# A mixed attention kernel on one core: score banks in groups of two instead of three and two, reciprocals moved to GpSimd, and a re-planned order of work

## The chip, the core and the metric

The kernel runs on one core of a Trainium2 chip, whose engines work side by side: TensorE (PE; its weight loads are PEld), VectorE (DVE), ScalarE (ACT), GpSimd (POOL) and SyncE (SP, which issues DMAs). TensorE writes into PSUM, which has eight banks of 512 float32 columns over 128 partitions. The metric is the device time of one execution in microseconds (us), as a median over runs.

## What is computed

Two attention branches over the same input x (2048 tokens, width 512, 32 heads of 16) are mixed by a gate. All data is bfloat16.

```python
g = sigmoid((x * gate_w).sum(-1, keepdims=True))
# branch A: softmax attention, per head, 2048 x 2048 scores
q, k, v = split(x @ A_wqkv)
a = (softmax(q @ k.T * 16 ** -0.5) @ v) @ A_wo
# branch B: linear attention with a feature map, per head
q, k, v = split(x @ B_wqkv)
phi = lambda t: concat(softmax(t @ w_phi), softmax(-(t @ w_phi)))
num = phi(q) @ (phi(k).T @ v)
den = phi(q) @ phi(k).sum(tokens) + 1e-6
b = (num / den) @ B_wo
out = g * a + (1 - g) * b
```

## The kernel before

**Branch A** is nearly all of the time. Its scores are cut into 2048 tiles of 128 keys x 512 queries of one head. Four heads lie in the four 32-row strips of TensorE, so a *pack* is the four tiles of one key block; there are 512 packs, and 16 packs in a row (all keys) make one *group* `g` of four heads and 512 queries. Each tile is scored (`_scores`, one matmul in one row strip, L931), exponentiated, and multiplied with the values (`_values`, one matmul in one column strip, L1034), where an extra column of ones gives the softmax denominators. All tiles of a group add into one PSUM bank `ot`.

The exponentials are shared between two engines. `NUMS` says how many tiles of each group go to VectorE (452 in all). ScalarE takes the rest (1596) as ACTIVATE with Exp (`_exp`, L978), out of a *ring* of PSUM banks (`NRING` = 5, banks 0 to 4). The groups of the ring alternate between three banks and two (`GROUPS` = (3, 2)). The score pass of ring group k (`_qk`) waits for the exponential k-2, which used the same banks. The first tiles go in two halves of 256 queries, so that ScalarE can start on half of the input. VectorE's tiles (`_vector_batch`, four at a time) are scored into banks of the *pool* (banks 5 to 7), turned into the bits of an exponential by one TENSOR_SCALAR each (L847), and refined by two additions for each batch (L864, one of 2048 columns and one of 4096). Each of these tiles costs four value matmuls instead of one, against `V` and a scaled copy `V2`.

A finished group is normalized in `_norm`: a transpose out of PSUM (L1055), multiplication of the denominators with the gate (L1062), reciprocal (L1064), product (L1067, on GpSimd where two groups go together, which is 15 times), transpose back (L1072).

**Branch B** is done in between, in `_branch_b`. `_b_pair` handles two token tiles at a time, 16 times: projections, a copy out of PSUM (L1160), negation (L1179), a tree of maxima (L1181, L1182), subtraction (L1184), exponential on ScalarE (L1187), a tree of sums (L1189, L1190, last L1192), reciprocal (L1200, `_b_rec`) and product (L1194). `_b_kv` sums keys with values, `_b_num` multiplies with the query features and divides (L1266, L1269, L1270, all VectorE). Projections of branch A (`_proj_k`, `_proj_q`, `_proj_v`, and for the first 512 tokens `_proj_k0`, `_proj_q0`) take pool banks too, except for the very first key and query projection, which go to banks 3 and 4. Query tiles are masked into two halves by GpSimd (L728), `V2` is made there too (L766).

**The order of the work** is made by a planner (`Plan`). Each operation has an engine, an estimated cost, a due time `prio`, an earliest time `rel` and dependencies; `order` goes through time and gives the next free engine the ready operation of least rank, with pool banks handed out on the way. The result is one fixed list for each engine; each engine then works its list strictly in order and waits on semaphores. `LAT` and `MORE` are the assumed delays between engines. An operation whose `urgent` time has come goes ahead of all others (`rank`). PE operations that would delay the next score pass are held back (`_late`). A score pass in the row strips can take along scores of VectorE's tiles in strips that are free (`_beside`). Where PE would be too idle, the planner inserts filler passes with zeros (`pad`, `filler`, L1041) and whole-array fillers ahead of score passes (L950, from score pass number 8 on); `SPAN`, `SHARE`, `GAPS`, `FLOOR`, `PAD` set when. Operations of GpSimd, and those of VectorE listed in `PORT`, are planned never to overlap.

Of the kernel before, what the change touches and what calls it, by code (L numbers as in the profile page):

```python
# [63 lines left out]
class Plan:  # L64
# [3 lines left out]
    MORE = {("ACT", "PE"): 0.09, ("ACT", "DVE"): 0.1, ("DVE", "PE"): 0.022}  # L68
# [3 lines left out]
    SPAN, SHARE, FILL = 2.4, 0.5, 0.2155  # L72
    PAD, PADS, OVER = 0.45, 2, 0.2
    SLIP, GAPS, FLOOR = 0, 0.6, 0.44
# [76 lines left out]
    NEAR = 0.2  # L151
    SAME = 16
    OPEN = 99
    HURRY, FREE = 20, 60
    PORT = ("v_step", "b_neg", "b_max", "b_sub", "b_sum", "b_mul", "n_mul", "n_den", "kvbd")
# [227 lines left out]
class _Kernel:  # L383
    NRING = 5
    GROUPS = (3, 2)
    NSLOT = 25
# [4 lines left out]
    KEEP = 15  # L391
    URGENT, AHEAD, SOON, REST = 5, -(1 << 30), 4, 6
    QDUE, KDUE, VDUE = 24, 17, 8
    P_Q, P_MUL, P_NEG = 1, 1, 0
    GDUE = 26
    VMIN = 12
    ALONE, EARLY = 9, 8
# [30 lines left out]
    def _memory(self, ctx):  # L428
# [13 lines left out]
        self.iden = sb("iden", [P, P], BF16)  # L442
# [3 lines left out]
        self.zero = sb("zero", [P, 32], BF16)  # L446
        self.warm = sb("warm", [P, QCH], BF16)
        self.gwb = sb("gwb", [P, 4, P], BF16)
        self.gh = sb("gh", [P, 2, NQC, 16], F32)
# [20 lines left out]
        self.bq = sb("bq", [P, self.NBQ, 2, 2 * D], BF16)  # L470
        self.btree = sb("btree", [P, 32, 8, 4], BF16)
        self.bsum = sb("bsum", [P, P], F32)
        self.brec = sb("brec", [P, P], FP16)
        self.kvacc = sb("kvacc", [P, 2, 260], F32)
# [71 lines left out]
    def _consts(self):  # L546
# [25 lines left out]
        op("POOL", lambda e: e.memset(self.zero[:], 0.0), 0.1, writes=[self.b_zero], prio=-75)  # L572
        self.b_wphi0 = B()
# [14 lines left out]
    def _projections(self):  # L588
# [12 lines left out]
        for j in range(NQC):  # L601
            if j == 0:
                for half, banks in enumerate(((3, 4), (None, None))):
                    self._proj_k0(half, banks[0])
                    self._proj_q0(half, banks[1])
            else:
                self._proj_k(0, j)
            self._proj_v(0, 4 * j)
            self._proj_v(0, 4 * j + 2)
# [63 lines left out]
    def _proj_k0(self, half, bank):  # L673
# [4 lines left out]
                   self.c_dve(256), 2 * half - 2.5, -99, "kproj", [self.b_k0[half]], n=256, bank=bank)  # L678

    def _proj_q0(self, half, bank):  # L680
# [4 lines left out]
        for c in range(4):  # L685
# [3 lines left out]
                   acquire=None if c else pool)  # L689
        for side in range(2):  # L690
# [48 lines left out]
    def _proj_v(self, pr, t0):  # L739
# [5 lines left out]
        for tt in range(2):  # L745
# [8 lines left out]
            mm.urgent = 64 * pr + t0 - self.SOON + 2  # L754
# [53 lines left out]
    NUMS = (4, 10, 12, 14, 14, 14, 14, 14, 14, 14, 14, 14, 15, 14, 16, 14, 13, 14, 15, 14, 17, 14, 15, 15, 14, 14, 11, 15, 21, 16, 21, 12)  # L808
# [134 lines left out]
    def _qk(self, a, b, half=None):  # L943
# [22 lines left out]
        o.pad = k >= 8  # L966
# [83 lines left out]
    def _norm(self, qc, src, side, last, dst, b_dst, due, job, alone=False):  # L1050
# [6 lines left out]
        if not (side or alone):  # L1057
# [4 lines left out]
        op("DVE", lambda e: e.tensor_tensor(rinv[:, lo:hi], den, h, ALU.mult), 0.23, reads=reads + [self.b_g],  # L1062
           writes=[b_rinv], name="n_den", prio=due)
        op("DVE", lambda e: e.reciprocal(rinv[:, lo:hi], rinv[:, lo:hi]), 0.2 + 0.1 * n, reads=[b_rinv],  # L1064
           writes=[b_rinv], name="n_rec", prio=due)
        spare = self.P_MUL and n == 2
        op("POOL" if spare else "DVE", lambda e: e.tensor_tensor(  # L1067
# [8 lines left out]
    NDUE = 26  # L1076
    K0, SK, Q0, SQ = 34.0, 12.0, 214.0, 14.25

    def _branch_b(self):
# [7 lines left out]
        self.b_kvbd, self.b_onB, self.b_rinvB = B(), [B(), B()], [B(), B()]  # L1087
        self.b_phiT = [B() for _ in range(4)]
# [58 lines left out]
    def _b_pair(self, s, t0, due):  # L1147
# [25 lines left out]
        def chain(ops, off, bufs):  # L1173
            for name, cost, fn in ops:
                spare = self.P_NEG and name == "b_neg"
                op("POOL" if spare else "DVE", fn, 1.35 if spare else cost, reads=bufs, writes=bufs, name=name,
                   prio=due + off)
        spread = lambda t: t[:, :, None, :].to_broadcast([P, 32, DH, 4])
        chain([("b_neg", 0.16 + 1024 * 0.00027, lambda e: e.tensor_scalar(both[:, :, 1], both[:, :, 0], -1.0, 0.0,  # L1179
                                                                         op0=ALU.mult, op1=ALU.add)),  # L1180
# [10 lines left out]
                                                                       half[:, :, n:2 * n], ALU.add)) for n in (4, 2)]  # L1191
              + [("b_sum", 0.3, lambda e: e.tensor_tensor(last(self.bsum[:]), half[:, :, 0], half[:, :, 1], ALU.add)),  # L1192
                 ("b_rec", 0.96, self._b_rec),
                 ("b_mul", two(2048), lambda e: e.tensor_tensor(x, x, spread(last(self.brec[:])), ALU.mult))],  # L1194
              2, [b, self.b_tree])
        return slot

    def _b_rec(self, e):
        with self.nc.allow_low_precision(reason="11 bits, each product is rounded to 8"):
            return e.reciprocal(self.brec[:], self.bsum[:])  # L1200
# [47 lines left out]
    def _b_num(self, t, due):  # L1248
# [4 lines left out]
        b_rinv.readers = []  # L1253
        for hf in range(2):
            job = Job()

            def mm(e, hf=hf, job=job):
# [6 lines left out]
            view = self._view17(job)  # L1264
            r = rinv[:, 16 * hf:16 * hf + 16]
# [7 lines left out]
                prio=due - 20, release=job))  # L1273
        b_rinv.readers = list(muls)
# [26 lines left out]
    def _out(self, qc):  # L1301
        op, NT, NQC = self.plan.op, self.NT, self.NQC
        for tt in range(4):
# [5 lines left out]
            if final:  # L1309
                due = self.NPACK  # L1310
                deps = (self.last_bits if tt < 2 else [self.pvs[-1]]) + [w for b in b_onTA[:3] for w in b.writers]
            else:
                deps = [w for b in b_onTA for w in b.writers]
            for x in first:
                x.prio, x.rel = due, due - (6 if not final else 8 if tt < 2 else 0)
                x.deps += deps
            m = first[-1]
# [58 lines left out]
```

## Time and profile before the change

| | |
|---|---|
| median of three runs | 772.22 us (771.98 to 772.43) |
| the profiled execution's own time | 772.22 us |
| its span, first to last instruction | 770.2 us |
| TensorE clock granted | 1.000 throughout |
| exponentials on ScalarE (L978) | 641: 318 of three banks, 318 of two, 5 small ones |
| exponentials of branch B on ScalarE (L1187) | 16 |
| tiles on VectorE (L847) | 452 |
| filler matmuls (L1041) | 760 |
| GpSimd busy | 57.9 us |

A page of the profile gives for each engine its busy time, share of the span and number of instructions; then groups of instructions by source line, as engine, operation, output<-inputs, shapes and count, followed by busy time, mean length of one in ns, idle time before them and what ended it. The chain that ended last is followed back from the last instruction: at each step to what released it or, where nothing did, to the instruction before it on its engine. A ScalarE instruction begins before the one ahead of it has ended, so the spans of neighbours overlap, and an engine may look busy while it waits.

### The profile page before, as it was taken

To read this page: it belongs to the slowest core of one execution; us is meant where nothing else is said; L and a number is where in the kernel's file an instruction comes from. 1 tells how busy PE (TensorE), PEld (TensorE's weight loads), DVE (VectorE), ACT (ScalarE), POOL (GpSimd) and SP (SyncE) were. 2 spreads that over 40 slices of the span, in tenths; PEclk is the share of its full clock that TensorE was granted. 3 is DMA by queue.
4 is the path that set the end of the run, shared out by engine and by line. 5 is a ranking of instruction groups with operands and counts; after the bars stand their busy time and mean duration, and the time that the engine had idled before them with its cause. 6 is when DMAs were issued, how large, how long until landed. Compare 5 with 4: busy or idle time off the path is not lost.

```text
span 770.2 us, 16369 instructions
## 1 busy us (share of the span) xinstructions
PE 747.0 (97%) x7126; PEld 231.5 (30%) x7126; DVE 725.3 (94%) x1207; ACT 755.1 (98%) x663; POOL 57.9 (8%) x73
## 2 busy tenths in 40 slices
PE   8999999999999999999999999999999999999998
PEld 4333333322322232222232223222323232322222
DVE  4789999999999999999999999999999999999994
ACT  6999999999999999999999999999999999999996
POOL 3200102000010100001001010000010101010000
PEclk9999999999999999999999999999999999999999
DMA  9510000000000000000111010102001110100000
GB/s 233 124 29 1 2 1 2 1 1 2 1 1 2 1 2 1 1 2 1 29 28 29 21 35 15 42 9 49 8 9 36 32 31 16 35 9 2 1 2 28
DMA packets 46456, 16.79 MB, mean 22 GB/s; under 512 B 40752, under 2 KB 45872, under 8 KB 46384
## 3 DMA queue, kind: packets, MB, share of 16 engines
q1 hardware_dynamic: 44512, 14.97, 9.1%
q8 instruction: 55, 0.90, 0.5%
q10 hardware_dynamic: 1872, 0.79, 0.4%
q14 instruction: 17, 0.14, 0.1%
HBM read 4.21 MB, written 2.10 MB: 8 GB/s over the span
## 4 chain that ended last, share of the span: by engine, by line
ACT 87%; PE 7%; DVE 5%; DMA 1%; SPq 0%; issue 0%
ACT ET L978 83%; ACT bq L1187 4%; PE ps L931 2%; PE ps L1034 2%; PE ps L640 2%; DVE vs L847 2%; DVE vs L864 1%; DMA xT<-in_A_x_dram 1%; DVE WB L1133 0%; DVE bq L1184 0%; PE ps L1041 0%; DVE bq L1160 0%; DVE btree L1182 0%; PE ps L749 0%; DVE ghB L802 0%; SPq L515 0%
## 5 line engine op out<-in xcount | busy, mean ns | idle before, releaser
L978 ACT ACTIVATE ET<-ps 128x1024 bf16<-128x1024 f32 (+2 forms) x641 | 725.7, 1340 | 2.4 <-PE ps L931 2.4
L931 PE MATMUL ps<-qT,kT 32*128 32x512 bf16 (+1 forms) x2053 | 304.9, 383 | 12.8 <-ACT ET L978 8.2
L847 DVE TENSOR_SCALAR vs<-ps 128x512 uint16<-128x512 f32 x452 | 297.4, 681 | 13.6 <-PE ps L931 11.9
L864 DVE TENSOR_SCALAR vs<-vs 128x2048 uint16<-128x2048 uint16 x226 | 214.8, 955 | 0.8
L1034 PE MATMUL ps<-ET,V 128*32 128x512 bf16 x1596 | 196.7, 387 | 0.1
L1034 PE MATMUL ps<-vs,V 128*32 128x512 bf16 x1808 | 179.9, 384 | 2.9 <-DVE vs L864 2.7
L931 PEld LDWEIGHTS ps<-qT,kT 32*128 32x128 bf16 x2053 | 76.9, 91 | 261.0 <-ACT ET L978 187.1
L1034 PEld LDWEIGHTS ps<-ET,V 128*32 128x32 bf16 x1596 | 49.9, 94 | 92.6 <-issue 79.7
L1041 PE MATMUL ps<-kT,zero 128*32 128x512 bf16 x760 | 75.1, 383 | 0.0
L1034 PEld LDWEIGHTS ps<-vs,V 128*32 128x32 bf16 x1808 | 45.1, 95 | 67.7 <-issue 31.3
L640 PE MATMUL ps<-WB,xT 128*128 128x512 bf16 x192 | 56.7, 384 | 0.4 <-DVE WB L1133 0.4
L728 POOL TENSOR_SCALAR qT<-qtmp,mask 128x512 bf16<-128x512 bf16 x30 | 25.6, 865 | 311.2 <-DVE qtmp L723 311.2
L1067 POOL TENSOR_TENSOR T<-T,rinv 128x512 bf16<-128x512 f32 x15 | 16.5, 1102 | 296.7 <-DVE rinv L1064 296.7
L640 PE MATMUL ps<-xT,WA 128*128 128x512 bf16 x120 | 35.8, 384 | 0.0
L1187 ACT ACTIVATE bq<-bq 128x2048 bf16<-128x2048 bf16 x16 | 31.5, 1970 | 0.4 <-DVE bq L1184 0.3
L1055 DVE STREAM_TRANSPOSE T<-ps 128x512 f32<-128x512 f32 x32 | 22.7, 710 | 7.7 <-PE ps L1034 7.2
L1041 PEld LDWEIGHTS ps<-kT,zero 128*32 128x32 bf16 x760 | 19.4, 95 | 18.9 <-issue 13.7
L1160 DVE CAST bq<-ps 128x512 bf16<-128x512 f32 x32 | 21.7, 683 | 2.2 <-PE ps L640 2.2
L640 PEld LDWEIGHTS ps<-WB,xT 128*128 128x128 bf16 x192 | 14.1, 97 | 27.3 <-issue 16.4
L1184 DVE TENSOR_TENSOR bq<-bq,btree 128x2048 bf16<-128x2048 bf16 x16 | 19.8, 1240 | 0.1
L1194 DVE TENSOR_TENSOR bq<-bq,brec 128x2048 bf16<-128x2048 bf16 x16 | 19.6, 1224 | 0.0
L640 PE MATMUL ps<-WoA,onTA 128*128 128x512 bf16 x64 | 18.7, 382 | 0.0
(75 smaller groups left out, 341.2 us busy)
## 6 DMA issues: line engine op xcount, KB each, us to landing
WB<-in_B_wqkv_dram SPq DMA_DIRECT2D x1, 1536.0 KB, 8.7
out_dram<-WB SPq DMA_DIRECT2D x12, 128.0 KB, 1.7
WA<-in_A_wqkv_dram SPq DMA_DIRECT2D x2, 384.0 KB, 4.5
WoB<-in_B_wo_dram SPq DMA_DIRECT2D x1, 512.0 KB, 3.8
WoA<-in_A_wo_dram SPq DMA_DIRECT2D x1, 512.0 KB, 4.8
WA<-in_A_wqkv_dram ACTq DMA_DIRECT2D x2, 128.0 KB, 3.0
WA<-in_A_wqkv_dram ACTq DMA_DIRECT2D x1, 256.0 KB, 4.2
WA<-in_A_wqkv_dram SPq DMA_DIRECT2D x1, 256.0 KB, 5.0
```

The source lines that it names most:

```text
L640: return e.matmul(out, lhs, rhs, start=start, stop=stop)
L728: x = self.plan.op("POOL", lambda e, side=side: e.tensor_scalar(self.qT[:, s0 + side, :], tmp, self.mask[:, side:side + 1], 0.0, op0=ALU.m ...
L847: parts.append(op("DVE", lambda e, j=j, job=job: e.tensor_scalar(va[:, 0, j, :], self._bank(job), SCALE * LOG2E * 128.0, float(ORIGIN), op ...
L864: o = op("DVE", lambda e, k=k, src=src, dst=dst: e.tensor_scalar(dst, src, float(STEPS[k - 1]), None, op0=ALU.add), 0.16 + k * n * QCH * 0 ...
L931: return e.matmul(out[:, cols], self.kT[32 * i:32 * i + 32, cp, kt * TOK:(kt + 1) * TOK], self.qT[32 * i:32 * i + 32, s, cols], start=True ...
L978: o = plan.op("ACT", lambda e: e.activation(self.ET[:, a % NS:a % NS + n, cols], self.ps[:, a % NR:a % NR + n, cols], ACT.Exp, scale=SCALE ...
L1034: ins = e.matmul(self._bank(ot)[32 * i:32 * i + 32, :], v[:, v0:v0 + 32], tile, start=(kt == 0), stop=(kt == self.NT - 1), tile_position=( ...
L1041: ins = e.matmul(self._bank(ot)[32 * i:32 * i + 32, :], self.zero[:], self.kT[:, 0, 0:QCH], start=False, stop=False, tile_position=(0, 32 ...
L1055: t1 = op("DVE", lambda e: e.transpose(T1[:, side].rearrange("p b s -> p (b s)"), src()), 0.735, deps=last, writes=[b_T1[side]], name="n_t ...
L1160: [lambda e, b, k=k: e.tensor_copy(bq[:, k].rearrange("p (g s v) -> p g s v", g=8, s=2)[:, :, 0, :], b.rearrange("p (g v) -> p g v", g=8))],
L1184: + [("b_sub", two(2048), lambda e: e.tensor_tensor(x, x, spread(tree[:, :, 0]), ALU.subtract))],
L1187: op("ACT", lambda e: e.activation(flat, flat, ACT.Exp), 1.8, reads=[b], writes=[b], name="b_exp", prio=due + 1)
```

## The change

- The ring shrinks from five banks to four, in groups of two and two; the pool has banks 4 to 7. The slots that hold exponentiated tiles are 24 instead of 25. The first four tiles, not five, go in halves. The very first key and query projections land in banks 3 and 2.
- `NUMS` gives VectorE 466 tiles.
- `_reciprocal` is new: seven GpSimd instructions (a first guess from the bits, then two rounds of multiply, scale-and-add, multiply). It replaces VectorE's reciprocal in `_b_pair` and, where two groups are normalized together, in `_norm`, where the product with the gate (L1062) moves to GpSimd too.
- In `_b_pair` the negation and the last sum (now `b_total`) run on GpSimd. With `P_SUM = 1` the two middle sums stay on VectorE, since the condition is `n <= P_SUM` for n of 4 and 2. With `P_BMUL = 0` the product stays as well.
- With `P_M = 0` the new GpSimd branch of `_b_num` isn't taken. `PADK = 8` is the score pass from which fillers may precede scores, as before. `LAST`, `FIRST_OUT`, `NEXT_OUT` and `DEP_OUT` have the values that the code had.
- `_proj_k0` and `_proj_q0` get an `urgent` time, so that the first keys and queries go ahead of other projections.
- Many numbers of the planner differ: delays (`MORE`), thresholds for fillers, due times of branch B, of the gate and of projections; `SAME` (the preference for staying in TensorE's row or column mode) goes from 16 to 100.

```diff
-    MORE = {("ACT", "PE"): 0.09, ("ACT", "DVE"): 0.1, ("DVE", "PE"): 0.022}
+    MORE = {('ACT', 'PE'): 0.21, ('ACT', 'DVE'): 0.1, ('DVE', 'PE'): 0.022, ('PE', 'DVE'): 0.027}
-    SPAN, SHARE, FILL = 2.4, 0.5, 0.2155
-    PAD, PADS, OVER = 0.45, 2, 0.2
-    SLIP, GAPS, FLOOR = 0, 0.6, 0.44
+    SPAN, SHARE, FILL = 3.0, 0.48, 0.2155
+    PAD, PADS, OVER = 0.45, 2, 0.1
+    SLIP, GAPS, FLOOR = 0, 0.7, 0.3
-    NEAR = 0.2
-    SAME = 16
+    NEAR = 0.1
+    SAME = 100
-    HURRY, FREE = 20, 60
+    HURRY, FREE = 10, 50
-    NRING = 5
-    GROUPS = (3, 2)
-    NSLOT = 25
+    NRING = 4
+    GROUPS = (2, 2)
+    NSLOT = 24
-    KEEP = 15
-    URGENT, AHEAD, SOON, REST = 5, -(1 << 30), 4, 6
+    KEEP = 13
+    URGENT, AHEAD, SOON, REST = 5, -(1 << 30), 6, 4
-    P_Q, P_MUL, P_NEG = 1, 1, 0
-    GDUE = 26
+    P_Q, P_MUL, P_NEG = 1, 1, 1
+    P_REC, P_SUM = 1, 1
+    P_M, P_BMUL, CHUNKS = 0, 0, 8
+    GDUE = 36
-    ALONE, EARLY = 9, 8
+    VSOON = 4
+    PADK = 8
+    LAST, FIRST_OUT, NEXT_OUT, DEP_OUT = 0, 8, 0, 2
+    ALONE, EARLY = 12, 5
...
-                for half, banks in enumerate(((3, 4), (None, None))):
+                for half, banks in enumerate(((3, 4) if self.NRING == 5 else (3, 2), (None, None))):
...
-                   self.c_dve(256), 2 * half - 2.5, -99, "kproj", [self.b_k0[half]], n=256, bank=bank)
+                   self.c_dve(256), 2 * half - 2.5, -99, "kproj", [self.b_k0[half]], n=256, bank=bank,
+                   urgent=3 * half - 99)
...
+            m.urgent = half - 99
...
-            mm.urgent = 64 * pr + t0 - self.SOON + 2
+            mm.urgent = 64 * pr + t0 - self.VSOON
...
-    NUMS = (4, 10, 12, 14, 14, 14, 14, 14, 14, 14, 14, 14, 15, 14, 16, 14, 13, 14, 15, 14, 17, 14, 15, 15, 14, 14, 11, 15, 21, 16, 21, 12)
+    NUMS = (4, 8, 12, 14, 14, 14, 17, 14, 14, 14, 14, 14, 17, 14, 16, 16, 13, 18, 15, 12, 18, 16, 17, 13, 16, 17, 9, 20, 22, 16, 15, 13)
...
-    NDUE = 26
-    K0, SK, Q0, SQ = 34.0, 12.0, 214.0, 14.25
+    NDUE = 23
+    K0, SK, Q0, SQ = 30.0, 12.0, 217.0, 14.25
...
+    def _reciprocal(self, s, guess, tmp, out, reads, bufs, prio):
+
+        n = s.shape[-1]
+        high = lambda a: a.bitcast(U16).rearrange("p (n two) -> p n two", two=2)[:, :, 1]
+        t, r = tmp[:, 0], tmp[:, 1]
+        do = lambda name, cost, fn: self.plan.op("POOL", fn, cost, reads=reads, writes=bufs, name=name, prio=prio)
+        do("r_bits", 0.17 + 0.001 * n, lambda e: e.tensor_scalar(
+            high(guess), high(s), -1.0, float(0x7EE0), op0=ALU.mult, op1=ALU.add))
+        for x, y, by, plus in ((guess, r, -1.2011100358638287, 2.192845599791731), (r, out, -1.0, 2.0)):
+            do("r_mul", 0.17 + 0.0019 * n, lambda e, x=x: e.tensor_tensor(t, s, x, ALU.mult))
+            do("r_rest", 0.17 + 0.001 * n, lambda e, by=by, plus=plus: e.tensor_scalar(
+                t, t, by, plus, op0=ALU.mult, op1=ALU.add))
+            do("r_step", 0.17 + 0.0019 * n, lambda e, x=x, y=y: e.tensor_tensor(y, x, t, ALU.mult))
```

## The prediction

> **What bounds the kernel now.** I read the page's busy times first, then the chain that ended last, then the groups of instructions, and only then the starts of single instructions.
>
> ```profile
> PE 747.0 (97%) x7126; PEld 231.5 (30%) x7126; DVE 725.3 (94%) x1207; ACT 755.1 (98%) x663; POOL 57.9 (8%) x73
> ...
> ACT 87%; PE 7%; DVE 5%; DMA 1%; SPq 0%; issue 0%
> ACT ET L978 83%; ACT bq L1187 4%; PE ps L931 2%; PE ps L1034 2%; PE ps L640 2%; DVE vs L847 2%; DVE vs L864 1%; DMA xT<-in_A_x_dram 1%; DVE WB L1133 0%; DVE bq L1184 0%; PE ps L1041 0%; DVE bq L1160 0%; DVE btree L1182 0%; PE ps L749 0%; DVE ghB L802 0%; SPq L515 0%
> ```
>
> Three engines look full, but 87% of the chain is ScalarE. PE's 97% contains 760 filler matmuls of L1041 (190 passes of four); VectorE is off the chain outside a few stretches. The chain in order of time (start, length, what) shows where:
>
> ```profile
> 13.41 28.15 ACT ET L978 x25
> 60.82 3.48 DVE WB L1133 x3
> ...
> 86.18 40.82 ACT ET L978 x36
> ...
> 258.98 1.79 DVE vs L847 x3
> 267.68 1.80 DVE vs L847 x3
> ...
> 650.07 97.19 ACT ET L978 x86
> 762.77 3.57 PE ps L640 x16
> ```
>
> 86 exponentials in 97.19 us are 1.130 us each, with nothing else on the chain. The groups, different shapes kept apart, give the two sizes:
>
> ```profile
> L978 ACT ACTIVATE ET<-ps 128x1536 bf16<-128x1536 f32 x318 | 494.5, 1555 | 0.4 <-PE ps L931 0.3
> L978 ACT ACTIVATE ET<-ps 128x1024 bf16<-128x1024 f32 x318 | 360.8, 1134 | 1.5 <-PE ps L931 1.5
> ```
>
> Their spans overlap, so a span is no price. From start to next start, in the trace, a three-bank one takes 1.331 us (the usual case, and within 1 ns the least) and a two-bank one 0.904; that is 0.051 us per instruction plus 0.4265 per bank. ScalarE's bare work is then 318 x 1.331 + 318 x 0.904 + 2.8 (five small ones) + 16 x 1.80 (L1187) = 742.4 us. The first exponential starts at 7.9 us, the last tile ends 8.3 us before the end of the span. 770.2 - 742.4 - 7.9 - 8.3 leaves **11.6 us lost**: 1.6 in one wait at 11.8 us (bank freed, scores late), and some 10 in small waits hidden inside the spans. That is all this change can win, apart from work it takes off ScalarE.
>
> **The change, part by part.** My sum is against the profiled execution: span 770.2, its own time 772.2, equal to the median of the three runs; 2.0 us lie around the span.
>
> *Groups of two, 466 tiles on VectorE.* ScalarE keeps 2048 - 466 = 1582 tiles instead of 1596. Four go in halves (4 x 0.477 us), 789 pairs take 0.904: 713.3 + 1.9 + 28.8 = 744.0 us, **+1.6**. In other words 152 more instructions at 0.051 cost 7.8, 14 tiles fewer save 6.0, the rest is the small ones. The Trainium skill, page "ScalarE: Activation LUTs", section "What ACT_TABLE_LOAD costs", speaks against the grouping more loudly: 186 ns plus 0.833 ns per element, with about 93 ns of overlap between neighbours, hence an estimated 93 ns fixed, by which 152 more would cost 14.1 us and the sum would be 6.3 us higher. The trace has 0.904 us as least and as median for a pair, which leaves 51 ns; I go by the trace.
>
> *The ring's rhythm.* A group may be scored again when the exponential two back has ended. From that end to the score matmul takes at least 55 ns, from the matmul to the exponential at least 438. After a three-bank exponential there are 1.331 + 0.904 - 1.555 = 0.680 us for this, so 187 ns to spare; after a two-bank one 2.235 - 1.134 = 1.101, so 608. With pairs it is 1.808 - 1.134 = 0.674 and 181 to spare, every time. Today the exponentials behind the tight case lose 22 ns each on average, the others 5 (without the wait at the start). If the tight case keeps its 22, 789 of them lose 17.4; if the easy case's 5 holds, 4. The planner's margin is larger now (it assumes 0.21 us more instead of 0.09 from ScalarE's end to PE, so it puts less PE work in front of a score), and VectorE and the bank pool get room, as worked out next. I take 6, nearer to the lower end, and keep 3 and 17 for the range.
>
> *VectorE's load.* Added: 14 tiles x (297.4 + 214.8)/452 = 15.9 us. Removed, by their rows: reciprocals of branch B 15.1 (L1200), of the softmax 5.1 (L1064, the 15 pairs), negation 6.6 (L1179), last sums 4.5 (L1192), denominators 3.0 (L1062): 34.3. Net **-18.4**, 725 to 707. None of it is on the chain except in the stretches near 60-84 and 257-274 us, where the trace has ScalarE's largest waits (0.3 to 0.5 us each, some 2 us in all). That is what it can win.
>
> *A fourth bank for everything else.* VectorE's waits for scores should fall. The waits (total us, times, longest):
>
> ```profile
> DVE vs L847 <- PE ps L931: 11.9, 29, 1.0
> PE ps L931 <- ACT ET L978: 8.2, 28, 0.7
> ```
>
> The first row is VectorE idle before a tile's conversion, off the chain; it is worth between 0 and the 1 to 2 us by which ScalarE then waits less.
>
> *PE.* 793 score passes instead of 641. In the starts a pass after a change between row and column mode follows 0.32 us after the one before, one in the same mode 0.22. So an added pass between column passes costs 0.43, 65 us for 152. Against that the VectorE tiles' own scores find two free row strips in every pass instead of one or two; today 232 of 873 row passes carry one tile. Some 80 of these saved at 0.22 give 18. Then there are 14 passes with values, 3. So PE gets 50 us more (33 to 68). It has 190 filler passes x 0.22 = 42 and some 75 us of gaps to take it from. It fits, at about 93%, and the cover is thin: were it gone, each microsecond would be ScalarE's.
>
> *GpSimd.* Its plain two-input row is 128x512 in 1056 ns, the one-input one 692:
>
> ```profile
> L728 POOL TENSOR_SCALAR qT<-qtmp,mask 128x512 bf16<-128x512 bf16 x30 | 25.6, 865 | 311.2 <-DVE qtmp L723 311.2
> L1067 POOL TENSOR_TENSOR T<-T,rinv 128x512 bf16<-128x512 f32 x15 | 16.5, 1102 | 296.7 <-DVE rinv L1064 296.7
> L1200 DVE RECIPROCAL brec<-bsum 128x128 f16<-128x128 f32 x16 | 15.1, 945 | 0.1
> ```
>
> The seven steps of a reciprocal over 128 elements are shorter than that; between a 205 ns memset (L554) and 692, I take 0.33 each: 2.3 us. With negation (1.3) and last sum (0.35) a pair of token tiles takes 4.0, a normalization 1.6: 16 x 4.0 + 15 x 1.6 = 88 us (50 to 180), POOL 58 to 146, idle four fifths of the time. The chain of a pair grows by about 2.5 us with its hand-overs; pairs come some 36 us apart, and VectorE has tiles to do meanwhile, so I cost it at nothing. If VectorE stands waiting for it instead, it is 16 x 2.5 = 40 us of VectorE, less the 18 won. Sharing costs something: L728's mean of 865 hides 692 in most and 1.2 to 1.7 where L864 ran beside it; L864's wide form went from 1217 to 1455 in five such cases, 2 us in all for 58 us of GpSimd. For 146 it is 5, taken from the 18. The Trainium skill, "GPSIMD Engine Reference", section "8. Key points", says that the two engines share SBUF interfaces in just such VectorE modes; the trace agrees (692 against 1730 at worst), and a kernel that hands GpSimd small work does pay.
>
> *First keys and queries first.* The second half's key projection now runs in front of the value projections. Today it waits behind 12 matmuls of L749, from 10.4 to 11.7 us; the exponentials stand still for 1.6 us. I take **-1.5** (0 to -2). Banks 2 and 3, where the first projections land, are now ring banks, which could give back some tenths.
>
> *What stays.* The pads' first pass is 8 as before; intermediate sums of 512 and 256 columns stay on VectorE (1 is below both widths); the numerators and the last output tiles keep their engines and due times. These parts are worth nothing. The tail of 8.3 us stays.
>
> Sum: 770.2 + 1.6 - 1.5 - (10 - 6) = 766.3, and 2.0 around it: **768.3 us**.
>
> **Rivals.** *(a) The forecast*, the waits shrink or stay near 10: 763 to 770.6, chance 0.52. *(b) It evens out*: waits stay at 9 to 11, the pads' and sums' parts do nothing, and extra instructions eat what the start wins: 772, chance 0.13. *(c) PE decides*: each pair needs its pass within 181 ns, a cycle of 0.904 holds one score pass and two column passes (0.32 + 0.32 + 0.22 = 0.86), a third makes 1.08. Where PE's work exceeds two column passes per pair, ScalarE waits: 22 ns for each gives 770.2 + 1.6 - 1.5 + 7.4 + 2.0 = 780, 40 ns 794. For it: 93% load, and 205 ns as upper quartile of the score's lateness today in the tight case. Against it: fillers can go, and the plan holds PE free in front of scores. It decides from about 15 ns lost per pair. Chance 0.26. *(d) GpSimd late*: VectorE behind a reciprocal for 16 x 2.5 us, net +22 us of VectorE, 747 of 754 available; the tiles come late and ScalarE loses 4 to 8: 777, chance 0.08. *(e) The dearer instruction* by that page's rule: 93 ns as a fixed part would make it 774.6; 311 pairs at 904 ns leave it 0.01.
>
> **The range.** Cutting (a) at 763.5 loses 0.06; the upper end at 780 leaves half of (c), 0.13. The measurement of this kernel tells 0.2%, 1.5 us: faster than 770.7 has 0.52, between 770.7 and 773.8 0.13, slower 0.35 (c, d, e). The forecast's own range is 763.5 to 770.6.
>
> **What would show it.** Right: some 793 exponentials of 0.904 start to start, the wait at 11.8 us gone, VectorE busy near 710, POOL near 145, fillers of L1041 well below 760, ScalarE over 86% of the chain. Wrong: PE's score rows with a larger share of the chain and ScalarE's starts at 0.93 or more (c); VectorE waiting for GpSimd by name (d). A start later than 7.9 us or a tail over 8.3 would break the frame of the sum.

## The result and the profile after

The changed kernel takes **776.83 us** (median of six runs, 775.8 to 777.35) against 772.22: the ratio is 1.0057, with a 95% interval of 1.0045 to 1.0070. It is slower by 0.57%; the forecast was 768.3. The profiled execution has a span of 775.0 us, 4.8 more than before, and a time of its own of 776.83.

First the page of the changed kernel: busy times, then the chain that ended last.

```profile
PE 763.5 (99%) x6859; PEld 211.3 (27%) x6859; DVE 715.7 (92%) x1151; ACT 758.1 (98%) x815; POOL 190.0 (25%) x340
...
ACT 83%; PE 15%; DVE 2%; issue 0%
ACT ET L996 79%; PE ps L949 5%; PE ps L656 4%; PE ps L1052 4%; ACT bq L1211 3%; PE ps L767 1%; DVE vs L865 1%; DVE vs L882 1%; PE ps L647 1%; PE ps L1152 0%; DVE bq L1230 0%; PE ps L664 0%; PE ps L703 0%; DVE kT L728 0%; ACT xT L1391 0%; PE ps L1059 0%
```

The lines have moved by some 18: the exponential is now L996, the score L949, the value pass L1052, VectorE's conversion L865 and its refinement L882. ScalarE issues 152 instructions more and is still most of the chain. PE has taken ground: the chain has 15% of it, against 7%. The exponentials and the waits for a freed bank, from the groups and the waits:

```profile
L996 ACT ACTIVATE ET<-ps 128x1024 bf16<-128x1024 f32 x789 | 730.3, 1283 | 3.5 <-PE ps L1052 2.6 <-PE ps L949 0.9
```

```profile
PE ps L949 <- ACT ET L996: 4.1, 17, 0.5
```

All exponentials but four are pairs, as forecast. PE's waits for ScalarE have halved (8.2 to 4.1 us). So the ring's rhythm did get easier, and the kernel got slower.

**Where the time went.** The prediction read ScalarE from start to start. The chain shows why that was wrong (start, length, what):

```profile
483.19 47.67 ACT ET L996 x52
...
532.64 45.83 ACT ET L996 x50
```

47.67/52 and 45.83/50 are 0.917 us per pair, with nothing else on the chain, where the least distance of two starts is 0.903. In a run of pairs the starts lie 0.903 to 0.904 apart while each span is some 13 ns longer than the one ahead; at about 1345 ns this stops, and from there the starts lie 0.917 apart too. The *ends* lie 0.917 apart all along. In the kernel before they do the same: 0.917 before a pair's end and 1.343 before a triple's, as median, with nine in ten within 2 ns of it. The mean of the two is 1.130, which is just what the prediction's own row gave (86 in 97.19 us) and what it took for 1.118 and a loss. So an instruction has a fixed part of 64 ns (0.917 - 2 x 0.4265), not 51, and the "hidden waits" were mostly ScalarE's own pace.

Counted from end to end, the span is the end of the first exponential, the work, what was lost between ends, and the tail:

| us | before | after | difference |
|---|---|---|---|
| first exponential ends | 8.72 | 9.07 | +0.35 |
| work: pairs 0.917, triples 1.343, branch B 1.789 each | 749.8 | 753.8 | +4.0 |
| lost before 26 us | 1.77 | 3.20 | +1.4 |
| lost later | 1.92 | 1.06 | -0.9 |
| last exponential's end to the end | 8.0 | 7.9 | -0.1 |
| span | 770.2 | 775.0 | +4.8 |

The work's difference is 152 instructions x 0.064 = +9.7 and 14 tiles x 0.4265 = -6.0, and some tenths for the small ones. Before the change only 1.9 us were lost after the start; that was all that a better rhythm could win.

The start is the other part. The stretches of the changed kernel, from 8 to 26 us and from 26 to 90 (length, then busy time of each engine):

```profile
8.00:26.00 18.00, 17.79 (x125) 7.55 (x122) 10.23 (x17) 14.73 (x18) 3.91 (x7) 1.00 1.04 237
26.00:90.00 64.00, 63.99 (x515) 18.24 (x514) 54.91 (x83) 64.00 (x71) 10.54 (x21) 1.00 0.10 26
```

ScalarE (fourth) is full from 26 us on. Before that PE (first) is, and ScalarE misses 3.3 us. The chain of that stretch is PE alone, score passes (L949) between projections (L767, L656) without a gap:

```profile
13.35 0.54 PE ps L656 x2
13.88 0.32 PE ps L949 x2
14.21 0.54 PE ps L767 x4
14.75 0.36 PE ps L949 x2
15.11 0.54 PE ps L767 x4
15.65 0.32 PE ps L949 x2
```

One pass of scores and one of projections, with the change between row and column mode, take 0.87 us, next to the 0.917 of a pair; when a second projection or a value pass comes in, ScalarE waits (1.3 us at 21.3 and 1.5 us at 24.7). In the kernel before, the chain is ScalarE alone from 13.41 to 41.56 us. In the changed kernel it stays with PE up to 89.5 us, although ScalarE loses nothing between 26 and 93 us: there the two engines run level, so PE might have held up a part of what a better start would win.

### The profile page after: what moved, and what is told of

Its sections match the earlier page's. It is cut to its first block, busy times and chain, and to the rows that moved or that the text cites. A ratio compares the mean times of both kernels' runs of the same rounds, so it can differ in the third digit from the quotient of the medians.

```text
span 775.0 us, 16189 instructions
## 1 busy us (share of the span) xinstructions
PE 763.5 (99%) x6859; PEld 211.3 (27%) x6859; DVE 715.7 (92%) x1151; ACT 758.1 (98%) x815; POOL 190.0 (25%) x340
## 4 chain that ended last, share of the span: by engine, by line
ACT 83%; PE 15%; DVE 2%; issue 0%
ACT ET L996 79%; PE ps L949 5%; PE ps L656 4%; PE ps L1052 4%; ACT bq L1211 3%; PE ps L767 1%; DVE vs L865 1%; DVE vs L882 1%; PE ps L647 1%; PE ps L1152 0%; DVE bq L1230 0%; PE ps L664 0%; PE ps L703 0%; DVE kT L728 0%; ACT xT L1391 0%; PE ps L1059 0%
## 5 line engine op out<-in xcount | busy, mean ns | idle before, releaser
L996 ACT ACTIVATE ET<-ps 128x1024 bf16<-128x1024 f32 (+1 forms) x793 | 732.5, 1279 | 4.2 <-PE ps L1052 2.6
L865 DVE TENSOR_SCALAR vs<-ps 128x512 uint16<-128x512 f32 x466 | 301.9, 680 | 19.5 <-PE ps L949 17.6
L949 PE MATMUL ps<-qT,kT 32*128 32x512 bf16 (+1 forms) x2052 | 314.2, 384 | 5.0 <-ACT ET L996 4.1
L882 DVE TENSOR_SCALAR vs<-vs 128x2048 uint16<-128x2048 uint16 (+2 forms) x234 | 222.8, 965 | 0.8
L1052 PE MATMUL ps<-vs,V 128*32 128x512 bf16 x1864 | 209.5, 385 | 0.7 <-DVE vs L882 0.6
L1052 PE MATMUL ps<-ET,V 128*32 128x512 bf16 x1582 | 193.3, 388 | 0.0
L949 PEld LDWEIGHTS ps<-qT,kT 32*128 32x128 bf16 x2052 | 78.0, 91 | 330.3 <-ACT ET L996 320.9
L1052 PEld LDWEIGHTS ps<-ET,V 128*32 128x32 bf16 x1582 | 46.9, 94 | 87.8 <-issue 83.4
L1217 POOL TENSOR_TENSOR bsum<-btree 128x128 f32<-128x128 f16 x16 | 12.1, 754 | 232.7 <-DVE btree L1214 232.7
L656 PE MATMUL ps<-WB,xT 128*128 128x512 bf16 x192 | 60.0, 385 | 0.2 <-DVE vs L865 0.2
L1052 PEld LDWEIGHTS ps<-vs,V 128*32 128x32 bf16 x1864 | 44.9, 95 | 50.7 <-issue 37.0
L1059 PE MATMUL ps<-kT,zero 128*32 128x512 bf16 x464 | 46.2, 382 | 0.0
L1202 POOL TENSOR_SCALAR bq<-bq 128x1024 bf16<-128x1024 bf16 x16 | 21.6, 1350 | 89.0 <-DVE bq L1184 69.7
L656 PE MATMUL ps<-xT,WA 128*128 128x512 bf16 x120 | 38.3, 385 | 0.0
L1081 POOL TENSOR_TENSOR rinv<-T,gh 128x32 f32<-128x32 f32 x15 | 5.4, 360 | 131.6 <-DVE T L1073 131.4
L746 POOL TENSOR_SCALAR qT<-qtmp,mask 128x512 bf16<-128x512 bf16 x30 | 25.8, 866 | 35.1 <-DVE qtmp L741 34.9
L1073 DVE STREAM_TRANSPOSE T<-ps 128x512 f32<-128x512 f32 x32 | 22.7, 708 | 10.3 <-PE ps L1052 10.1
L1184 DVE CAST bq<-ps 128x512 bf16<-128x512 f32 x32 | 21.8, 681 | 0.4 <-PE ps L656 0.3
L784 POOL TENSOR_SCALAR V<-V 128x544 bf16<-128x544 bf16 x16 | 12.1, 754 | 36.8 <-DVE V L777 36.6
L656 PEld LDWEIGHTS ps<-WB,xT 128*128 128x128 bf16 x192 | 13.4, 97 | 26.0 <-issue 19.7
L777 DVE CAST V<-ps 128x512 bf16<-128x512 f32 x16 | 11.1, 691 | 9.9 <-PE ps L767 9.8
```

The costliest lines, as they stand in the source:

```text
L656: return e.matmul(out, lhs, rhs, start=start, stop=stop)
L746: x = self.plan.op("POOL", lambda e, side=side: e.tensor_scalar(self.qT[:, s0 + side, :], tmp, self.mask[:, side:side + 1], 0.0, op0=ALU.m ...
L865: parts.append(op("DVE", lambda e, j=j, job=job: e.tensor_scalar(va[:, 0, j, :], self._bank(job), SCALE * LOG2E * 128.0, float(ORIGIN), op ...
L882: o = op("DVE", lambda e, k=k, src=src, dst=dst: e.tensor_scalar(dst, src, float(STEPS[k - 1]), None, op0=ALU.add), 0.16 + k * n * QCH * 0 ...
L949: return e.matmul(out[:, cols], self.kT[32 * i:32 * i + 32, cp, kt * TOK:(kt + 1) * TOK], self.qT[32 * i:32 * i + 32, s, cols], start=True ...
L996: o = plan.op("ACT", lambda e: e.activation(self.ET[:, a % NS:a % NS + n, cols], self.ps[:, a % NR:a % NR + n, cols], ACT.Exp, scale=SCALE ...
```

## The experiments

Theory F: ScalarE is the bound, at a fixed 64 ns per instruction measured at the ends; the change costs what its instructions cost, less the tiles, plus a start in which PE's scores come late. Its rivals put the loss elsewhere: in GpSimd's chains (theory G), in VectorE, in PE's passes (theory P), or (theory S) in the slots for exponentiated tiles, 24 instead of 25, which hold up the start. "Work" and "lost" below are counted at the ends, as in the table. Five rounds each; the kernel before took 772.34 to 772.44 beside them. Some of these kernels let the planner make its lists anew, and then one edit brings others with it; it is said where.

**split.** The kernel before, its triples issued as two instructions, two banks and one. All lists stay.

```diff
-        o = plan.op("ACT", lambda e: e.activation(
+        def act(e):
+            for x, m in ((a, 2), (a + 2, 1)) if n == 3 and half is None else ((a, n),):
...
+        o = plan.op("ACT", act,
```

> The kernel before, in which each three-bank exponential is issued as two instructions (two banks, then one) over the same data; the planned order of all engines is the same. 316 more ScalarE instructions, nothing else. Theory F (ScalarE's own work bounds both kernels, and its true cadence is read from end to end: 1.343 and 0.917 us, so 64 ns fixed per instruction): +20 us, 792. With the 51 ns that the prediction took from starts: +16, 788. Theory P (ScalarE mostly waits for scores, rival c): the extra instructions fall into the waits, +8 at most, under 781. An overlap estimate of 93 ns fixed would give +29, 801.

791.0 us, ratio 1.0244 (1.0230 to 1.0257). Work 769.9 (+20.1), lost 2.4 (-1.3), span 789.3 (+19.1). ScalarE's line on the page counts the instructions:

```profile
PE 740.9 (94%) x7067; PEld 230.0 (29%) x7126; DVE 731.6 (93%) x1207; ACT 774.3 (98%) x981; POOL 58.0 (7%) x73
```

981 against 663 are 318 more, so the work grew by 63 ns and the span by 60 ns for each; at the forecast's 51 ns the work would have grown by 16.2. The fixed part is 64 ns within 1, and hardly any of it is absorbed.

**ring4_only.** The kernel before with the ring of four, groups of two and 24 slots alone (and the first projections in banks 3 and 2); new lists.

```diff
-    NRING = 5
-    GROUPS = (3, 2)
-    NSLOT = 25
+    NRING = 4
+    GROUPS = (2, 2)
+    NSLOT = 24
...
```

> The kernel before with the ring of four banks in groups of two and 24 slots alone: 452 tiles, VectorE's reciprocals, the planner's numbers of before (it makes new lists). Theory F (ScalarE's own work): 156 more exponentials than before at 64 ns, +10: 782, with its end-to-end work near 760. If the fourth pool bank pays by itself: 775 or less. Theory P (scores late in every pair): 788 or more, with the loss beside the work grown by 6 or more.

785.46 us, ratio 1.0167 (1.0153 to 1.0181). Work 760.2, that is +10.4 for 159 more instructions (65 ns each); lost 7.2, of which 3.2 before 26 us. The grouping by itself costs 13 us, four fifths of it plain instructions. Theory F had expected 782; the rest is waits. The change's new numbers and its 14 tiles win 8.6 of that back, 6.4 of it as work.

**gp_only.** The kernel before with GpSimd's parts alone: reciprocals, negation, last sums, denominators.

```diff
-    P_Q, P_MUL, P_NEG = 1, 1, 0
+    P_Q, P_MUL, P_NEG = 1, 1, 1
+    P_REC, P_SUM = 1, 1
```

> The kernel before with GpSimd's parts alone (negation, last sums, denominators, reciprocals): ring of five, 452 tiles, the planner's numbers of before, new lists. Theory F: ScalarE's work is that of before, so 772 within 1.5, although VectorE has 34 us less to do. If VectorE's relief pays by itself: 770 or less. Theory G (GpSimd's chains late): 775 or more.

774.81 us, ratio 1.0028 (1.0017 to 1.0038). Work unchanged, 749.8; lost 5.5 instead of 3.7. VectorE is relieved (707.9 busy, GpSimd 187.7) and it pays nothing: time taken off an engine that is off the chain is only worth what is then done with it. The time lies above theory F's 772 within 1.5 and just under the 775 of late GpSimd chains. The lists are new here, so the 1.8 us of loss are not put down to one cause.

**short_exp** and **short_before.** The changed kernel, and the kernel before, with exponentials of 496 of 512 columns, so that ScalarE has 21 us less work; but for one memset on GpSimd, which fills the columns left out with zeros, nothing else changes.

```diff
-        cols, w = (slice(0, QCH), QCH) if half is None else (slice(256 * half, 256 * half + 256), 256)
+        cols, w = (slice(0, QCH - 16), QCH) if half is None else (slice(256 * half, 256 * half + 256), 256)
...
```

> The changed kernel whose exponentials on ScalarE leave out the last 16 of 512 queries of each tile (their slots stay zero), all lists as in the changed kernel: 789 x 32 x 0.833 ns = 21.0 us less ScalarE work, nothing else. Theory F: nearly all of it comes back, 756 to 762. Theory P (scores, PE): 5 at most, 772 or more. In between: ScalarE bounds, with PE or VectorE close behind.

> The kernel before whose exponentials leave out the last 16 of 512 queries of each tile, lists as before: 1591 x 16 x 0.833 ns = 21.2 us less ScalarE work. The changed kernel gave back 16.0 of 21.0. Theory F: the same here, 755 to 757. If the kernel before had more cover on PE (ring of five): more than 17 come back, 754 or less; if VectorE with its fuller load stops it earlier: under 12, 760 or more.

The changed kernel takes 760.81 us, ratio 0.9845 (0.9832 to 0.9859): 16.0 of 21.0 us come back, so ScalarE was its bound. The kernel before takes 765.56, ratio 0.9923 (0.9911 to 0.9936): only 6.9 of 21.2 come back, where theory F had expected 755 to 757; the rival, VectorE with its fuller load, had 760 or more. The chains by engine, short_exp first, short_before second:

```profile
PE 42%; DVE 34%; ACT 21%; POOL 1%; DMA 1%; issue 0%; SPq 0%
```

```profile
PE 46%; DVE 41%; ACT 12%; DMA 1%; issue 0%; SPq 0%
```

In both, PE and VectorE take over. In the kernel before they stood 7 us behind ScalarE, in the changed one 16. So the change did make the room in PE and VectorE that it was forecast to make; it lay behind an engine that had become dearer.

**dve_more.** The changed kernel with each of the 32 copies of branch B's projections (L1184) made twice; lists otherwise the same.

```diff
+            for e, names in (('DVE', ('pq_ev',)),):
...
+                        x = Op(e, o.fn, o.cost, "again", o.prio, -99, o.kind, o.lat)
...
```

> The changed kernel with the 32 copies of branch B's projections out of PSUM made twice by VectorE, lists otherwise the same: 21.8 us more VectorE, about what the move to GpSimd had taken off. Theory F: VectorE has room at these places, 776.8 to 779. If the relief of VectorE was what paid for 14 more tiles: 785 or more, since the lists are made for the shorter work.

789.63 us, ratio 1.0223 (1.0209 to 1.0236), 12.8 us above the changed kernel. 21.8 us were added to VectorE; some 9 of them found room. Lost 17.1, all over the kernel, in pieces of 0.1 to 0.8 us after the start. Theory F's 776.8 to 779 failed here, and the rival's 785 or more came: with some 22 us more, about what the move to GpSimd had taken off it, VectorE is no longer hidden behind ScalarE.

**gp_twice.** The changed kernel with five of the seven instructions of each GpSimd reciprocal made twice; lists otherwise the same.

```diff
+            for e, names in (('POOL', ('r_bits', 'r_mul', 'r_step')),):
...
```

> The changed kernel with five of the seven GpSimd instructions of each reciprocal issued twice, one after the other, all lists otherwise the same: about 69 us more GpSimd work and the chains of branch B and of the normalizations longer by 1.5 to 3 us. Theory G (GpSimd's chains or its sharing with VectorE cost the time): 780 or more. Theory F (ScalarE's own work): 776.8, at most 778.

831.29 us, ratio 1.0759 (1.0736 to 1.0783). GpSimd's busy time goes from 190 to 252, and 61.7 us are lost. Two stretches show how (length; busy PE, PEld, DVE, ACT, POOL; the clock granted to TensorE):

```profile
270.00:290.00 20.00, 19.91 (x171) 5.36 (x168) 19.51 (x32) 20.00 (x22) 11.04 (x24) 1.00 0.00 1
290.00:350.00 60.00, 56.07 (x474) 13.86 (x470) 46.18 (x71) 49.44 (x53) 16.53 (x35) 0.80 0.01 1
```

From 270 to 290 us ScalarE is full. Then waits follow and the clock falls. The longest wait, 2.4 us, ends at 323.9 us: the chain before it runs through the doubled steps of one reciprocal from 314.98 to 320.78 us, then through the product that VectorE makes of it. From 326 to 340 us, at a clock of 0.54, ScalarE ends a pair every 1.51 us instead of 0.917, ten times over, before it recovers. GpSimd now has 15% of the chain (POOL in the page's row by engine), and VectorE waits 25.8 us for reciprocals. Theory F had at most 778 here, theory G 780 or more. Yet in the kernel as it is GpSimd is in time: VectorE waits 0.3 us for it in all. What the run shows is that its chains can't take twice the steps, and that a stall costs far more than itself.

**dve_recip.** The changed kernel with negation, sums, denominators and reciprocals back on VectorE, 466 tiles kept; new lists.

```diff
-    P_Q, P_MUL, P_NEG = 1, 1, 1
-    P_REC, P_SUM = 1, 1
+    P_Q, P_MUL, P_NEG = 1, 1, 0
+    P_REC, P_SUM = 0, 0
...
```

> The changed kernel with negation, last sums, denominators and reciprocals back on VectorE, all else as changed. Theory F: ScalarE is the bound and VectorE has room to 96%: 776.8 within 1.5. Theory G (GpSimd late or in VectorE's way): faster by 2 or more, 774 or less. If VectorE's freed time matters: slower by 2 or more.

815.82 us, ratio 1.0544 (1.0504 to 1.0584). Work the same, 753.8; lost 24.4 in the profiled execution (805.5 span), small until 460 us and then up to 11.0 at once, at 751.7; and the tail after the last exponential is 18.6 us instead of 7.9. Theory F's 776.8 within 1.5 failed, and "slower by 2 or more", the sign that VectorE's freed time matters, came. In these lists VectorE does not get through 466 tiles in time without GpSimd's help. With gp_only this speaks for one reading: GpSimd's part allows the 14 tiles, and only they earn.

**no_filler.** The changed kernel without its fillers; the order of all else the same.

```diff
+                    if o.name == "pad":
+                        continue
-            for _ in range(o.filled):
+            for _ in range(0):
...
```

> The changed kernel without its filler passes, lists otherwise the same: 116 passes of four filler matmuls and the whole-array fillers are left out, some 25 us of PE. Theory P (PE's score passes come late, rival c): 5 us faster or more. Theory F: within 1 of 776.8, as long as the granted clock stays; a lower clock would make it slower under both.

782.35 us, ratio 1.0135 (1.0109 to 1.0161). In the profiled execution (785.46 us) ScalarE's waits up to 370 us are those of the changed kernel; then come five stretches with waits of 0.59 us per pair. The granted clock, in 40 slices, shows where:

```profile
PEclk9999999999999999999899999999999999799999
```

Filler passes, then, were not what delayed ScalarE: leaving them out saved nothing, and cost where the clock fell (mean 0.98).

**slots28.** The changed kernel with 28 slots; the lists are made as for 24, so they stay the same and only waits for a slot go.

```diff
-    NSLOT = 24
+    NSLOT = 28
+    PLANNED = 24
...
```

> The changed kernel with 28 slots for exponentiated tiles instead of 24; the lists of all engines are those of the changed kernel, since the plan is still made for 24 and only the waits on slots are set afterwards (small buffers share memory to make room). Theory S (the waits of 1.3 and 1.5 us at 20 and 24 us are exponentials without a free slot, which the first value passes give back too late): both go, about 774. If these two starts waited for scores: no change, 776.8.

776.8 us, ratio 1.0056 (1.0043 to 1.0069). Lost 4.5, of which 3.1 at the start: the two waits became three, 1.1 us at 22.6, 0.4 at 23.9 and 1.1 at 26.0. Theory S falls: the trace named the value pass L1052 as what released the slot, but behind it stood PE, which had as much to do as before.

**start_swap** and **start_early.** The kernel before; the key projection of the second half ahead of the values' (the change's intent at the start), and in the second kernel five score passes moved forward past value and key projections as well.

```diff
+            ahead(p.queues["PE"], "kproj", 7, None)
+            ahead(p.queues["DVE"], "kproj_ev", 1, "vproj_ev")
```

```diff
+            for name, nv in (("qk5", 1), ("qk6", 3), ("qk8", 5), ("qk9", 7)):
+                o = next(o for o in q if o.name == name)
+                v = [x for x in q if x.name == "vproj"][nv]
...
```

> The kernel before with its lists kept but for two places: the last matmul of the second half's first key projection stands ahead of the twelve matmuls of value projections, and its copy ahead of the first value copy. The one start wait of 1.57 us should go: 770.7, and all else as before. If PE is the bound there anyway, the wait only moves: 772.3.

> The kernel before with the change of the swap (second half's last key matmul and its copy early) and five score passes, the sixth to the tenth, moved one place forward past value and key projections; all else as in its lists. If the start wait of 1.6 us is PE's list order, so that scores stand behind projections whose results nobody needs yet: it goes, 770.8. If PE is full there whatever the order: 772.3, the wait moves to about 15 us.

772.48 us, ratio 1.0000 (0.9991 to 1.0009), and 772.07, ratio 0.9996 (0.9988 to 1.0005). Lost at the start 1.6 and 1.5, against 1.8 before. In start_swap the wait stays where it was and is 1.4 us long: the score pass still stands behind the same projections. In start_early that wait is gone, and 1.3 us are lost between 15 and 18.6 us instead, where PE's chain has no gap. So the wait of 1.6 us at 11.8 us that the forecast wanted to win is not a matter of order alone: PE is full, and moving score passes moves the wait.

**soon.** The changed kernel with two margins smaller, by which projections go ahead of other work before they are needed; new lists.

```diff
-    URGENT, AHEAD, SOON, REST = 5, -(1 << 30), 6, 4
+    URGENT, AHEAD, SOON, REST = 5, -(1 << 30), 4, 4
-    VSOON = 4
+    VSOON = 2
```

> The changed kernel with the two due margins of key and value projections at the old values (SOON 4 and VSOON 2 instead of 6 and 4). The first value pass then stands one score pass earlier in PE's list, in front of eight matmuls of value projections. Theory S (the two waits of 1.3 and 1.5 us at 20 and 24 us come from exponentials that wait for a free slot, so for the first value passes): both go, 774. If they come from late keys instead: they stay, 776 to 777.5.

778.51 us, ratio 1.0087 (1.0072 to 1.0102). That is neither of the two times expected. The start loses 0.6 instead of 3.2, so its waits belong to this order of the work and not to pairs as such; but the profiled execution loses more elsewhere (2.7 us at 136, and nearly 4 between 387 and 394, where the granted clock was 0.57). It took 782.58 us, 4 more than the median, so the second of these losses need not be in the others. The run shows that a start without the waits can be had, not what it is worth.

**half_values.** The changed kernel without half of the value projections of the first 16 heads.

```diff
-                for c in range(4):
+                for c in range(4) if pr else (0, 3):
```

> The changed kernel with half of the value projections of the first sixteen heads left out (two of four matmuls for each of the eight double tiles, 32 matmuls of 256 columns, 3.5 us of PE between 8 and 30 us), lists otherwise the same. If the start's 3.1 us are PE full of projections: the waits at 20 and 24 us shrink to under 1 in all, 774. If they come from keys, slots or VectorE: 776.5.

778.44 us, ratio 1.0083 (1.0064 to 1.0102). Inconclusive: in the profiled execution (780.28 us), with less PE work, the clock fell to 0.52 between 12 and 26 us, so that the passes that were left took longer, and the start lost 4.9 us. The shortest of the six, 776.23 us at a mean clock of 1.000, lies inside the changed kernel's own range; there too the 774 that was expected of a start full of projections did not come, but no trace of it was kept.

**ring5.** The changed kernel with the ring of five and groups of three and two back, 466 tiles kept; new lists.

```diff
-    NRING = 4
-    GROUPS = (2, 2)
-    NSLOT = 24
+    NRING = 5
+    GROUPS = (3, 2)
+    NSLOT = 25
```

> The changed kernel with five ring banks in groups of three and two and 25 slots, all else as changed (466 tiles, GpSimd's parts, planner's numbers). Theory F: ScalarE loses 152 instructions at 64 ns, 9.7 us: about 767 if the start stays as in the changed kernel, and faster than both kernels if VectorE keeps up with three pool banks. Theory P: the easy rhythm returns for half of the groups, the waits in the steady part shrink, a gain of 5 to 10 as well, but then the steady waits, end to end, must have been there before: they would be near zero by F. Theory G (GpSimd's reciprocals late): no better than the kernel before, 772 or more.

1171.7 us as the median of six (1145 to 1179); the ratio of 1.493 (1.485 to 1.501) is that of the two shortest, 1145 and 1161. Theory F had expected about 767. The work is 743.5, 10.3 less than with pairs, as F has it, but 385 us are lost: the lists fall apart, ScalarE waits 233 us for value passes and VectorE 210 us for scores, at a clock of 0.845. It says nothing on what pairs cost in the changed kernel; it says that with these planner numbers three pool banks don't carry 466 tiles.

## Why the prediction was wrong

The sign was wrong. 776.83 lies inside the wide range of 763.5 to 780 only because that kept half of rival (c), whose mechanism made at most the 1.4 us at the start; it lies outside the forecast's own range of 763.5 to 770.6. By its own steps:

- **What bounds the kernel now, and the ring's rhythm: this step failed.** "From start to next start ... 1.331 ... 0.904; that is 0.051 us per instruction" took the starts for the pace. The pace is 1.343 and 0.917. The starts gave a warning that was read over: 234 of the 318 pairs, not 311, lie at 904 or 905 ns, and 74 of the 318 triples at 1347 or 1348. Of the "11.6 us lost", 318 x (0.012 + 0.013) = 8 us were ScalarE's work; 3.7 were lost, 1.8 of them at the start. The gain of 10 - 6 = 4 us could not exist; measured are 0.9. That the waits get shorter was right: in the changed kernel three quarters of the scores follow the freed bank within 57 ns, and 1.1 us are lost in all after 26 us.
- **Groups of two, 466 tiles: the term was mis-sized**, +1.6 against +4.0, by the same 13 ns for 152 instructions and some tenths. ring4_only and split give the 64 ns twice more. So rival (e), the dearer instruction, which got a chance of 0.01, had the direction right, though not the size. The Trainium skill's "ScalarE: Activation LUTs", section "What ACT_TABLE_LOAD costs", whose 186 ns less an overlap of 93 had made the estimate of 774.6, came nearer to the time than the forecast, but by luck: by its 93 ns the work would grow by some 8, and the runs have +4.0. The measured 64 lies between the page's figure and mine.
- **First keys and queries first: this step failed**, -1.5 forecast, +1.4 measured (and 0.35 from a later first exponential, whose start varies from run to run, 7.9 to 8.5 us over the kernels with these lists). In the list made without the urgent times the order of PE is the same and on VectorE two neighbouring copies change places, so that edit did next to nothing; no run tried it alone. start_early shows that the wait at 11.8 us is PE's load, and start_swap that the key projection in front does not remove it. Rival (c)'s mechanism, a third pass that doesn't fit in a pair's cycle, cost time in the first 26 us; after them ScalarE lost 1.1 us in all.
- **VectorE's load: right that it is off the chain, its size was off.** Busy time fell by 9.6, not 18.4 - 5. The lengths of its instructions add up to 810.5 us before, in 725.3 busy: on VectorE too neighbours overlap. gp_only takes 29.4 us of lengths away and 17.4 of busy time. Rows were summed as prices here as well.
- **GpSimd: 190 instead of 146, still hidden.** A pair of token tiles takes 5.8 instead of 4.0 (negation 1.35, last sum 0.75 and not 0.35, the reciprocal 3.7 and not 2.3). The trace of one line gives the reason (least, median, greatest length):

```profile
L1243 POOL TENSOR_TENSOR newton<-bsum,guess x16: 452/456/1304, 85.3 to 675.8; 128x128 f32<-128x128 f32 x16
```

  Thirteen of the 16 take 0.45 to 0.46; the three that begin together with a 4096-column form of L882 on VectorE take 1.30, and the mean is 0.61. By the prediction's own two numbers, five times 1455 less 1217 ns, the sharing that it put at 2 us comes to 1.2. Rival (d) didn't come: VectorE waits 0.3 us for GpSimd. But "I cost it at nothing" rested on a cover that gp_twice and dve_more show to be thin.
- **PE: right that it fits, wrong in size.** "50 us more" had 80 row passes saved; nearly all scores of VectorE's tiles ride along now (25 passes with a single tile, against 232), and there are 821 row passes instead of 873. It fits with 116 filler passes left of 190.
- **A fourth bank: the direction of VectorE's waits was wrong**, 17.6 us for scores instead of 11.9, off the chain as said. ring5 suggests that the bank matters to this order all the same.
- **The frame held but for the start.** The first exponential begins at 8.48 us and not by 7.9, which the prediction had named as a break of its sum. Of this delay 0.35 us is left at the end of the first exponential, which is shorter than before. The tail is 7.9 us, against 8.0 before by the same count. The parts that "stay" cost nothing visible.

As a whole: GpSimd's relief makes room on VectorE, the room takes 14 tiles (6.0 us), the grouping that goes with it costs 9.7 us of instructions, and the new order of the work 1.4 at the start. At 64 ns, 152 instructions need 23 tiles to be paid for; each tile costs VectorE 1.1 us (the 512 us of its two rows by 452), so nine more need 10 us, about what dve_more found to be free. That the change could therefore at best have broken even is argued, not tried. What stays open is the start: soon shows that the two waits can go, but no run has them gone and all else kept, so their 1.4 us are located, not recovered.

## What to carry to other kernels

Read the pace of a pipelined engine from end to end, or from a long unbroken row of the chain (length by count), before anything is called a hidden loss: starts can run ahead and spans overlap, and 13 ns misread 640 times made 8 us that were not to be won. Where an engine is the bound, count its instructions as well as its elements: merging or splitting tiles has a price per instruction that must be paid by work taken off the same engine. Time freed on an engine off the chain, and a wait removed where the feeding engine is full, come to nothing by themselves.

## What the hardware showed that was not expected

- The span of back-to-back ACTIVATEs grows by 13 ns each, up to about 1345 ns for a pair whose pace is 917; so a mean span (1134 before, 1283 after, for the same shape) says how long a run has been unbroken, not what an instruction costs.
- Less PE work can be slower. Without fillers the clock fell to 0.98 on average, with half of some projections left out to 0.99, and in such a stretch ScalarE lost 0.59 us per pair; with doubled GpSimd instructions the clock was 0.945, and the one late chain cost 2.4 us at 323.9 us and 6.0 more in ten such pairs. The clock stayed at 0.54 through these 14 us although the trace shows TensorE busy all the time.
- Small GpSimd instructions vary by a factor of three with what VectorE does beside them (0.456 us beside L865, 1.30 when they begin together with a 4096-column L882, for 128x128 f32).
